# A decode attention block on one core: the exps' own semaphore, the first exps placed behind the second pair's evictions, and TensorE's loop placed at a slot of a fetch block

## The chip, the cores and the metric

The kernel runs on one core of one Trainium2 chip. The metric is the device time of one execution in microseconds. The core has five engines that run their own instruction streams side by side and wait for one another through semaphores: TensorE (PE in the profile; PEld is its weight load), VectorE (DVE), ScalarE (ACT), GpSimd (POOL) and SyncE (SP, which here only issues transfers). 16 DMA engines move the data. Data lie in SBUF (128 partitions), matmul results in PSUM banks.

## The reference

One decode step: 8 sequences with one new token each, 32 heads with a cache of 4096 keys and values of 128 numbers, and a small MLP beside the attention. All inputs are bf16.

```
xn = layernorm(x)                                  # x: 8 x 1 x 640
q  = (xn @ wq) as 8 x 32 x 1 x 128
p  = softmax(q . k_cache * 128**-0.5)              # over 4096 keys, each head of each sequence
o  = p . v_cache, as 8 x 1 x 4096
h  = gelu(layernorm(xn) @ w1 + b1)
out = x + o @ wo + h @ w2 + b2
```

Nearly all of the work is reading the two caches: 8 x 32 x 4096 x 128 numbers of 2 bytes each, that is 268 MB of keys and as many of values.

## The kernel before

**Pairs.** The caches are worked through in 32 pairs, numbered `i` from 0 to 31. A pair is one sequence and 8 heads. Its keys are 8 MB and are spread over the 128 partitions: 16 partitions for each head, 256 keys of 128 numbers on each partition. Its values have the same layout. There are two key buffers (even and odd pairs) and one value buffer. Before the pairs stand the two layernorms, the query projection and the MLP, whose weights and results use parts of the same buffers.

**What one pair does.** The scores of the first 176 keys of a partition are made on VectorE in three chunks (`dve_chunk`): multiply by the query, add the two halves, reduce. The scores of the last 80 are made on TensorE in ten groups of 8: `pe_T` transposes 8 blocks of keys into PSUM, `act_T` evicts the group to SBUF on ScalarE (tile KT_sb), `pe_QK` multiplies it by the queries (tile S_ps), and `dve_sel` picks each partition's own head from the result. `dve_max` finds the maximum and writes the bias NB. Then `act_exp` computes 8 exps on ScalarE (one for each head, tile P_sb, with their sums), `pe_RS` adds the sums over partitions, and `pe_PV` is the value product: 256 matmuls, each with its own weight load, summed in PV_ps. `act_O` copies the result out and `o_norm` divides on GpSimd. At the end `fin_wo` multiplies by the output weights in four parts, the first two of them ahead of the last value product.

**Order.** Every step is put on a time line by hand: `at(position, function, pair)`, 100 positions to a pair, and the calls are sorted by position. Within one engine the order of positions is the order of instructions. For pair i (o = 100 i) the transposes, evictions and score products stand at o to o + 42, the exps at o + 90, and the row sums and the value product at o + 148 and o + 150, that is behind the score products of pair i + 1. On TensorE one turn thus holds, in this order, the score products of pair i + 1 and then the value product of pair i.

**Transfers.** All cache loads are issued from SP's queue, in the order keys i + 1, values i, keys i + 2, values i + 1. `load_k(i)` waits until pair i - 2 is done with its buffer (transposes and VectorE's chunks). `load_v(i)` waits for the value product of pair i - 1 (`tk[("pv", i - 1)]`), as there is one value buffer. SP waits in order, so a load that waits holds back those behind it. The values of the last pair come in four parts.

**Semaphores.** Each engine has one counting semaphore (`act_s` for ScalarE), raised by the instructions that others wait for. A wait is left out where the waiting engine has already waited for a later count of the same semaphore (class `_Eng`). TensorE has a second semaphore for the row sums and the value products (`pe2`).

**Loops.** VectorE and ScalarE have pairs 2 to 31 as a loop of 15 turns (`_replay_loop`). TensorE has a loop of 32 turns over pairs (`_replay_pe`): from turn to turn the instructions must be the same and the waited counts must grow by one step. A turn has a first half (query matmul, transposes and score products of the next pair; in the last turn, under `If_eq`, two parts of the output product instead) and a second half (row sums, value product). To keep the counts of `act_s` regular from the first turn on, the kernel before has two copies that no one reads: `act_exp(-1)` writes oU_sb, and `act_qbc(32)` writes qbc_sb.

**The first pairs.** Pair 0's score products stand ahead of TensorE's loop; the loop's first turn holds pair 1's score products and pair 0's value product. On ScalarE the exps of pair 0 stood at position 90, ahead of pair 1's evictions at 100 to 142.

Of the kernel before, what the change touches and what calls it, by code (L numbers as in the profile page):

```python
# [11 lines left out]
ACT = mybir.ActivationFunctionType  # L12
# [92 lines left out]
def _emit(e, call, wait=None, turn=None):  # L105
    name, a, k, inc = call
    a = [x.at(x.i if turn is None else turn) if isinstance(x, _Slot) else x for x in a]
    if name == "wait_ge":
        e.wait_ge(a[0], a[1] if wait is None else wait, **k)
        return  # L110
    inst = getattr(e, name)(*a, **k)  # L111
    if inc is not None:
        inst.then_inc(*inc)


def _replay(e, calls):
    for call in calls:
        _emit(e, call)
# [10 lines left out]
def _steps(turns):  # L129

    body = turns[0]
    assert len({len(t) for t in turns}) == 1, [len(t) for t in turns]
    grow = []
    for j, (name, args, kw, inc) in enumerate(body):
        step = 0
        for r in range(1, len(turns)):
            name_r, args_r, kw_r, inc_r = turns[r][j]
            assert name_r == name and inc_r == inc and sorted(kw_r) == sorted(kw), (j, name, name_r)
            if name == "wait_ge":
                assert args_r[0] is args[0]  # L140
                if r == 1:
                    step = args_r[1] - args[1]
                assert args_r[1] == args[1] + r * step and args[1] > 0 and step >= 0, (j, args, args_r)
            else:
                assert [_same(x) for x in args_r] == [_same(x) for x in args], (j, name)
                assert [_same(kw_r[x]) for x in sorted(kw)] == [_same(kw[x]) for x in sorted(kw)], (j, name)
        grow.append(step)
    return grow
# [14 lines left out]
def _replay_pe(e, calls, head, mid, end, late):  # L163

    n = len(head)
    first = [calls[a:b] for a, b in zip(head, mid)]
    second = [calls[a:b] for a, b in zip(mid, head[1:] + [end])]
    g1, g2 = _steps(first[:-1]), _steps([[c for c in t if not _late(c, late)] for t in second])
    _replay(e, calls[:head[0]])
    with e.bass.Fori(1, n + 1, engines=OrderedEngineSet([e.engine])) as r:  # L170
        reg = e.to_reg(r)
        with e.If_lt(reg, n):
            for call, step in zip(first[0], g1):
                _emit(e, call, call[1][1] + (r - 1) * step if step else None, r)
        with e.If_eq(reg, n):
            _replay(e, first[-1])
        g = iter(g2)
        for call in second[0]:
            if _late(call, late):
                e.wait_ge(call[1][0], (r >> (n.bit_length() - 1)) * 16 + 1)  # L180
            else:
                step = next(g)
                _emit(e, call, call[1][1] + (r - 1) * step if step else None)
    assert n & (n - 1) == 0
    _replay(e, calls[end:])


def _late(call, late):
    return call[0] == "wait_ge" and any(call[1][0] is x for x in late)


def bass_parallel_sum__gqa_block_cached__mixer_channel_mlp__decode_kernel(
# [17 lines left out]
    HS = 8  # L210
# [3 lines left out]
    NQ = NHQ * B  # L214
# [14 lines left out]
    def jp_of(i):  # L229
        return 80  # L230
# [16 lines left out]
    with ExitStack() as es:  # L247
# [3 lines left out]
        sem = lambda name: es.enter_context(nc.semaphore(name))  # L251
# [38 lines left out]
        qbc_sb = sb("qbc_sb", [P, 2, DH], BF)  # L290
        oT_sb = sb("oT_sb", [P, H, B], BF)
        oU_sb = sb("oU_sb", [P, 2, HS], F32)
        ident_bf = sb("ident_bf", [P, P], BF)
        mask_sb = sb("mask_sb", [P, HS], F32)
        off_sb = sb("off_sb", [P, HS], F32)
# [25 lines left out]
        assert H * B + (FB + 1) * B <= 384  # L321

        pe, dve, act, sp, pool = (_Eng(sem(f"{n}_s")) for n in ("pe", "dve", "act", "sp", "pool"))
        pe2 = _Eng(sem("pe2_s"))
        ld_s = [_Dma(sem(f"ld_s{s}")) for s in range(3)]
        ld_x, ld_b1, ld_b2, ld_wq, ld_w1, ld_w2a, ld_w2b, st_o = (
            _Dma(sem(n)) for n in ("ld_x", "ld_b1", "ld_b2", "ld_wq", "ld_w1", "ld_w2a", "ld_w2b", "st_o"))
# [3 lines left out]
        tk = {}  # L331
        prog = []

        def at(pos, fn, *a):
            prog.append((pos, len(prog), fn, a))
# [161 lines left out]

        def act_qbc(i):
            act.wait(tk.get(("ym", i - 2)))
            if i == NQ:  # L500
                act.sig(act.activation(qbc_sb[:, i % 2, 0:HS], off_sb[:, :], ACT.Copy))
                return
            QBB.use(act)
            tk[("qb", i)] = QBB.used(act, act.sig(act.activation(
                qbc_sb[:, i % 2, :], QB_ps[:, 0:DH], ACT.Copy)))
# [83 lines left out]

        def act_exp(i):  # L590
            s = i % 2
            if i < 0:
                act.wait(tk["mask"])
                act.sig(act.activation(oU_sb[:, s, :], off_sb[:, :], ACT.Copy))
                return
            act.wait(tk[("nb", i)], tk.get(("pv", i - 1)))
            for h in range(HS):
                last = act.activation(P_sb[:, h, :], Sd_sb[:, s, :], ACT.Exp, bias=NB_sb[:, s, h:h + 1],
                                      scale=SCALE, accum_out=rs_sb[:, h:h + 1])
            tk[("exp", i)] = act.sig(last)  # L600

        def pe_RS(i):
            pe.wait(tk[("exp", i)])
# [24 lines left out]

        def act_O(i):
            if i < 0:  # L630
                tk[("oU", i)] = PVB.used(act, act.sig(act.activation(oU_sb[:, i % 2, :], off_sb[:, :], ACT.Copy)))
                return
            PVB.use(act)
            tk[("oU", i)] = PVB.used(act, act.sig(act.activation(oU_sb[:, i % 2, :], PV_ps[:, 0:HS], ACT.Copy)))
# [42 lines left out]
        Q = 100.0  # L677
# [22 lines left out]
        for i in range(NQ):  # L700
            o = i * Q
            last = i == NQ - 1
            if i:
                at(o - 51, load_k, i)
            at(o + 50, load_v, i)
            at(o - 52, qrep, i)
            at(o - 2, k_ready, i)
            at(o - 11, pe_qbc, i)
            at(o - 10.5, act_qbc, i)
            nt = jp_of(i) // TPB  # L710
            w = 42.0 / nt
            for t in range(nt):
                at(o + w * t, pe_T, i, t)
                at(o + w * (t + 0.4), act_T, i, t)
                at(o + w * (t + 1.5), pe_QK, i, t)
            at(o + 2, dve_chunk, i, 0)
            at(o + 26, dve_chunk, i, 1)
            at(o + 52, dve_sel, i, 0)
            at(o + 55, dve_sel, i, 1)
            at(o + 58, dve_chunk, i, 2)  # L720
            at(o + 84, dve_max, i)
            at(o + 90, act_exp, i)
            at(o + Q + 48, pe_RS, i)
            at(o + Q + 57, dve_rinv, i)
            at(o + Q + 50, pe_PV, i)
            if not last:
                at(o + Q + 71, act_O, i)
            at(o + Q + 75, o_norm, i)
        at(-10, act_exp, -1)
        at(NQ * Q - 10.5, act_qbc, NQ)  # L730
        at(57, dve_rinv, -1)
        at(71, act_O, -1)
        at(75, o_norm, -1)
        o = NQ * Q
# [32 lines left out]
        @block.tensor  # L767
        def _(e):
            _replay_pe(e, pe.calls, head, mid, end[0], [d.sem for d in ld_vl])
# [40 lines left out]
```

## Time and profile before

| what | value |
|---|---|
| timed runs, us | 1292.55, 1292.06, 1290.01 (median 1292.06) |
| the profiled execution, us | 1290.35, with a span of 1288.5 |
| granted TensorE clock, mean | 0.576 |
| busy, share of the span | PE 52%, DVE 85%, ACT 37%, POOL 6% |
| DMA | 551.99 MB, mean 428 GB/s |
| chain that ended last | DMA 78%, PE 18%, ACT 1%, DVE 1% |

The span runs from the first instruction to the last; the execution's time has a little more around it. The chain is followed back from the last instruction, at each step to what released it. "issue" is time in which an engine waited for nothing that the profile shows. Value loads take 75% of the chain and value products 17%. An engine may be idle or busy without any effect on the time where it isn't on that chain, and a chain may run through work that another wait would replace at once.

Instruction fetches of TensorE show as a queue of their own (q8) in the table of DMA queues. All engines' program lines carry the number of the one line that replays the recorded calls, so groups are told apart by the tile that they write.

### The profile page before, as it was taken

Reading aid. Unit: us, or ns where it says so; the run is one execution under the profiler, and the core shown is the slowest. Engines: PE = TensorE matmul, PEld = TensorE weight load, DVE = VectorE, ACT = ScalarE, POOL = GpSimd, SP = SyncE. Lnnn points to the kernel's source line nnn. Section 1 sums busy time; section 2 is a strip of 40 time slices with the busy share of each in tenths; the row PEclk is TensorE's granted clock in tenths of the full one; section 3 lists DMA queues with packets and bytes.
Section 4 is the critical chain, followed back from the end, with each engine's and each line's share of the span. In section 5 each row is a group of like instructions: output and inputs, shape, how many; then the busy total and the mean of one; then the engine's idle time right before and its main releaser. Section 6 shows DMA issues by size and latency. Waiting matters only on the chain.

```text
span 1288.5 us, 34287 instructions
## 1 busy us (share of the span) xinstructions
PE 672.9 (52%) x13904; PEld 573.5 (45%) x13904; DVE 1089.4 (85%) x663; ACT 475.4 (37%) x906; POOL 77.4 (6%) x107
## 2 busy tenths in 40 slices
PE   4346544664544664544664644664644654544654
PEld 4235443553443553433553533553534543534544
DVE  1899888988888988888988888988888988888983
ACT  1344423344423344423344423344423344423341
POOL 0000000000000000000000000000000000000000
PEclk9955555666656666555565555556555665556565
DMA  9998999999999999999999999999999999999998
GB/s 398 443 425 373 446 433 423 442 437 423 431 448 423 427 452 423 423 454 425 423 454 425 423 450 429 423 442 437 423 434 444 425 429 446 427 425 450 427 402 347
DMA packets 14547, 551.99 MB, mean 428 GB/s; under 512 B 1276, under 2 KB 5445, under 8 KB 5574
## 3 DMA queue, kind: packets, MB, share of 16 engines
q1 hardware_dynamic: 14464, 551.79, 99.4%
q8 instruction: 9, 0.15, 0.0%
q10 hardware_dynamic: 70, 0.03, 0.0%
q14 instruction: 4, 0.03, 0.0%
HBM read 551.80 MB, written 0.01 MB: 428 GB/s over the span
## 4 chain that ended last, share of the span: by engine, by line
DMA 78%; PE 18%; ACT 1%; DVE 1%; issue 1%; SPq 0%; POOL 0%; ACTq 0%; DVEq 0%
DMA S_sb<-in_A_v_cache_dram 75%; PE PV_ps L111 17%; DMA S_sb<-in_A_k_cache_dram 3%; PE TR_ps L111 1%; ACT KT_sb L111 1%; DVE S_sb L111 0%; DVE Sd_sb L111 0%; PE S_ps L111 0%; ACT P_sb L111 0%; SPq L111 0%; PE ACC_ps L111 0%; PE CH_ps L111 0%; DVE S_ps L111 0%; DVE mx_sb L111 0%; PE QB_ps L111 0%
## 5 line engine op out<-in xcount | busy, mean ns | idle before, releaser
L111 PE MATMUL TR_ps<-ident_bf,S_sb 128*128 128x128 bf16 (+1 forms) x2570 | 339.9, 276 | 381.9 <-POOL kr_sb L111 367.4
L111 DVE TENSOR_TENSOR S_sb<-S_sb,qbc_sb 128x7552 bf16<-128x7552 bf16 (+1 forms) x96 | 388.8, 4050 | 143.7 <-DMA S_sb<-in_A_k_cache_dram 143.5
L111 PEld LDWEIGHTS TR_ps<-ident_bf,S_sb 128*128 (+2 forms) x2570 | 244.0, 103 | 439.4 <-issue 364.6
L111 DVE TENSOR_REDUCE Sd_sb<-S_sb 128x59 f32<-128x3776 bf16 (+1 forms) x96 | 390.2, 4065 | 3.3
L111 ACT ACTIVATE KT_sb<-TR_ps 128x1024 bf16<-128x1024 bf16 x320 | 326.9, 1023 | 124.1 <-PE TR_ps L111 112.6
L111 PE MATMUL PV_ps<-P_sb,S_sb 128*128 128x8 bf16 x8192 | 225.5, 175 | 157.8 <-DMA S_sb<-in_A_v_cache_dram 149.1
L111 PEld LDWEIGHTS PV_ps<-P_sb,S_sb 128*128 128x128 bf16 x8192 | 222.3, 103 | 161.0 <-DMA S_sb<-in_A_v_cache_dram 152.2
L111 ACT ACTIVATE P_sb<-Sd_sb,NB_sb 128x256 bf16<-128x256 f32 x256 | 126.2, 494 | 224.6 <-DVE NB_sb L111 224.6
L111 DVE TENSOR_TENSOR S_sb<-S_sb 128x3776 bf16<-128x3776 bf16 (+1 forms) x96 | 202.9, 2114 | 3.3
L111 ACT ACTIVATE oU_sb<-PV_ps 128x8 f32<-128x8 f32 x31 | 5.5, 177 | 403.8 <-PE PV_ps L111 403.8
L111 PE MATMUL S_ps<-qrep_sb,KT_sb 128*128 128x8 bf16 x2560 | 122.0, 177 | 41.8 <-ACT KT_sb L111 38.3
L111 PEld LDWEIGHTS S_ps<-qrep_sb,KT_sb 128*128 128x128 bf16 x2560 | 91.5, 102 | 73.3 <-ACT KT_sb L111 40.0
L111 POOL TENSOR_TENSOR oT_sb<-oU_sb,ri_sb 128x8 bf16<-128x8 f32 x31 | 60.5, 1953 | 397.8 <-ACT oU_sb L111 381.2
L111 ACT ACTIVATION_READ_ACCUMULATOR P_sb<-Sd_sb,NB_sb 128x1 f32 x256 | 47.7, 186 | 0.0
L111 POOL COPY qrep_sb<-qT_sb 128x128 bf16<-128x128 bf16 x32 | 12.8, 399 | 461.1 <-PE S_ps L111 441.4
L111 DVE TENSOR_REDUCE Sd_sb<-S_ps 128x40 f32<-128x320 f32 x64 | 31.5, 492 | 2.2
L111 DVE TENSOR_TENSOR S_ps<-S_ps,mask_sb 128x320 f32<-128x320 f32 x64 | 31.4, 490 | 1.7 <-PE S_ps L111 1.7
L111 POOL MEMSET kr_sb<- 128x1 f32 x32 | 3.1, 98 | 323.2 <-DMA S_sb<-in_A_k_cache_dram 323.2
L111 PE MATMUL CH_ps<-rs_sb,ones_f 128*128 128x8 f32 x64 | 16.0, 323 | 11.0 <-ACT P_sb L111 7.1
L111 PEld LDWEIGHTS CH_ps<-rs_sb,ones_f 128*128 128x128 f32 x64 | 13.2, 257 | 14.0 <-issue 14.0
L111 PE MATMUL CH_ps<-S_sb 128*128 128x8 bf16 (+1 forms) x244 | 12.0, 181 | 5.4 <-DMA S_sb<-in_A_wq_dram 4.7
L111 ACT ACTIVATE qbc_sb<-QB_ps 128x128 bf16<-128x128 f32 x32 | 8.9, 277 | 16.1 <-PE QB_ps L111 16.1
(46 smaller groups left out, 104.6 us busy)
## 6 DMA issues: line engine op xcount, KB each, us to landing
S_sb<-in_A_wq_dram SPq DMA_DIRECT2D x1, 5120.0 KB, 15.6
S_sb<-in_A_k_cache_dram SPq DMA_DIRECT2D x1, 4448.0 KB, 43.1
S_sb<-in_A_k_cache_dram SPq DMA_DIRECT2D x1, 3744.0 KB, 33.1
S_sb<-in_A_v_cache_dram SPq DMA_DIRECT2D x1, 3072.0 KB, 12.8
S_sb<-in_A_wo_dram SPq DMA_DIRECT2D x1, 2560.0 KB, 32.5
S_sb<-in_A_v_cache_dram SPq DMA_DIRECT2D x1, 2560.0 KB, 18.5
S_sb<-in_B_w_dram SPq DMA_DIRECT2D x1, 2160.0 KB, 20.2
S_sb<-in_B_w_dram SPq DMA_DIRECT2D x1, 2080.0 KB, 25.2
```

Source lines behind the costliest of these rows:

```text
L111: inst = getattr(e, name)(*a, **k)
```

## The change

The loop of TensorE gets a fixed place: its first instruction is put at slot 100 of a block of 256 instructions. The exps signal on a semaphore of their own, `act2_s`, through a second recorder `act2`; they are still recorded in ScalarE's stream, in the same order as its other calls. The exps of pair 0 move from position 90 to position 145, that is behind the evictions of pair 1; those of the other pairs stay at o + 90. The two copies that no one reads go, and the wait for the mask that the first of them held moves to `act_O(-1)`.

```diff
-    with e.bass.Fori(1, n + 1, engines=OrderedEngineSet([e.engine])) as r:
+    with e.bass.Fori(1, n + 1, engines=OrderedEngineSet([e.engine]), head_slot={e.engine: 100}) as r:
...
-        pe2 = _Eng(sem("pe2_s"))
+        pe2, act2 = _Eng(sem("pe2_s")), _Eng(sem("act2_s"))
...
         def act_qbc(i):
             act.wait(tk.get(("ym", i - 2)))
-            if i == NQ:
-                act.sig(act.activation(qbc_sb[:, i % 2, 0:HS], off_sb[:, :], ACT.Copy))
-                return
             QBB.use(act)
...
         def act_exp(i):
             s = i % 2
-            if i < 0:
-                act.wait(tk["mask"])
-                act.sig(act.activation(oU_sb[:, s, :], off_sb[:, :], ACT.Copy))
-                return
             act.wait(tk[("nb", i)], tk.get(("pv", i - 1)))
             for h in range(HS):
                 last = act.activation(P_sb[:, h, :], Sd_sb[:, s, :], ACT.Exp, bias=NB_sb[:, s, h:h + 1],
                                       scale=SCALE, accum_out=rs_sb[:, h:h + 1])
-            tk[("exp", i)] = act.sig(last)
+            tk[("exp", i)] = act2.sig(last)
...
         def act_O(i):
             if i < 0:
+                act.wait(tk["mask"])
                 tk[("oU", i)] = PVB.used(act, act.sig(act.activation(oU_sb[:, i % 2, :], off_sb[:, :], ACT.Copy)))
                 return
...
-            at(o + 90, act_exp, i)
+            at(o + 90 if i else o + Q + 45, act_exp, i)
...
-        at(-10, act_exp, -1)
-        at(NQ * Q - 10.5, act_qbc, NQ)
```

## The prediction

> **What bounds the kernel now.** I read the page's slices and queues first, then the chain of waits, the timelines of the queues, and a table of short windows.
>
> ```profile
> DMA  9998999999999999999999999999999999999998
> q1 hardware_dynamic: 14464, 551.79, 99.4%
> q8 instruction: 9, 0.15, 0.0%
> ```
>
> ```profile
> 105.94 21.78 DMA S_sb<-in_A_v_cache_dram
> 127.72 0.05 issue
> 127.77 7.04 PE PV_ps L111 x256
> 134.82 31.63 DMA S_sb<-in_A_v_cache_dram
> 166.45 0.05 issue
> 166.50 7.04 PE PV_ps L111 x256
> ```
>
> The transfers bound it: 551.79 MB keep the DMA engines busy 99.4% of the span. The second fence is the chain (start, length): value load, value product, next value load. A steady pair takes 38.70 us (134.82 to 173.55 and on), half of it, 19.35 us, for each 8 MB load. The chain seems to say that TensorE's 7.04 us matter. They don't: a value load issued onto a dry queue at 105.94 landed 21.78 us later, one issued at 134.82 needed 31.63 us, since a key load stood ahead of it. So each steady value load is issued 31.63 - 21.78 = 9.85 us before it is needed. Nothing TensorE, ScalarE or VectorE gains in a steady pair counts; only a dry queue does. There is one, at the fourth slice:
>
> ```profile
> 72.47 4.04 ACT P_sb L111 x16
> 76.52 0.92 ACT KT_sb L111
> ...
> 89.17 0.34 issue
> 89.52 0.59 PE CH_ps L111 x2
> 90.11 0.75 PE PV_ps L111 x28
> 90.86 4.63 issue
> 95.49 3.57 PE PV_ps L111 x128
> 99.06 4.01 issue
> 103.07 2.85 PE PV_ps L111 x100
> ```
>
> ```profile
> 100.00:102.00 2.00, 0.00 (x0) 0.50 1.11 467
> 102.00:104.00 2.00, 0.93 (x34) 0.50 0.15 66
> 104.00:106.00 2.00, 1.91 (x72) 0.50 0.03 8
> 106.00:108.00 2.00, 1.53 (x10) 0.50 1.55 524
> ```
>
> The first is the chain again: the first value product is broken twice by "issue", time in which TensorE waited for no semaphore: 4.63 us after 28 matmuls, 4.01 us after 128 more. 128 matmuls with their weight loads are 256 instructions, and the instruction queue q8 moved 0.15 MB in 9 packets, 16 KB each, 64 bytes for each of 256: TensorE ran out of code at two block boundaries. In the second fence (window, length, PE busy, granted clock, share of packets begun, GB/s) few packets begin between 102 and 106: key load 2 (issued at 70.88) is done, and value load 1 is issued only at 105.94, after the broken product.
>
> **Size of the hole.** Value load 1 landed at 127.72. The last part of key load 2 landed at 105.02 (landing events). Without a hole value load 1 ends 105.02 + 19.35 = 124.37: 3.35 us to be had on the engine that is last; the first engines were done at 103.09 and lost up to 4.76. Taking the busy time of packets in half-microsecond steps from 102 to 108, 3.4 of 16 engines' us are missing. From 21.78, the load must be issued by 124.37 - 21.78 = 102.59 to close the hole.
>
> **The change, part by part.**
>
> *The first exps behind the second pair's evictions.* Today ScalarE starts exp 0 at 72.47 (when VectorE has NB) and the 10 evictions of pair 1 wait behind it until 76.42, though their keys are there at 66.33 and TensorE has two transposed groups ready. Moved, pair 1's transposes, evictions and score products run at once. A steady pair needs 13.95 us from the keys' signal to the last score product (POOL's signal 147.13, its next copy 161.08). So the last score product ends at 66.33 + 13.95 = 80.3 instead of 89.17, and the last eviction at about 79.9. Behind it stand the eight exps, 4.04 us, and perhaps the exps' table load, 1.28 us (today at 60.43, in idle time): done at 83.9 to 85.2. I take 85.2. Who waits for them: the row sums and the product on TensorE, and VectorE's exp waits two pairs on, which come after 106. Value load 0, issued at 32.00, lands 53.6 us later, at 85.6. So data allow the product at about 85.8, 4.3 us earlier than today's 90.11.
>
> *TensorE's code.* Fetches of the instruction queue begin at 86.0, 93.0, 100.5 and 104.2; each takes 1.0 to 1.1 us. The first block boundary inside the product was free 95.49 - 89.2 = 6.3 us after the block before was entered, the second 103.07 - 95.49 = 7.6 us; so one block is fetched ahead, on entering a block, and takes a mean of 6.94 us while loads fill the engines. A block of product runs 3.57 us. Counting the records of one turn, there are 673 instructions from the loop's head to the product's first, with 242 skipped ones (output weights), and 515 from there to the loop's end. Head at slot 100: 100 + 673 = 773 = 3 x 256 + 5, so the product does begin a block, to within my count; today, 57 instructions ahead of a boundary, the head is at about slot 38. But 513 instructions of product begun at slot 0 to 5 don't end in two blocks: the last few stand in a third. The block before the product is entered by pair 1's last score product, about 12 instructions before the first half ends, at 80.0. Then: first product block 80.0 + 6.94 = 86.9 (after exps and data, so it decides), second 93.9, third 100.8, end 100.9. Bounds by 6.3 and 7.6: 98.9 and 102.8; where the third isn't needed, 93.9 + 3.6 = 97.5. I take 100.9, as the count puts instructions in the third block. That is ahead of 102.59 by 1.7 us: the hole closes, with 0.2 us left at the far bound. The placement itself gains nothing then: with the boundaries where they are today, the chain would be two fetches and 100 matmuls, 80.4 + 2 x 6.94 + 2.85 = 97.1.
>
> The Trainium skill, "Runtime: NRT & Kernel Launch", section "Instruction fetch mechanics", says that code is fetched ahead in 16 KiB blocks and that crossing a block is mostly hidden. Here the blocks agree, and 4.63 and 4.01 us of stall say that it isn't hidden under full loads. By that rule the product would run from 85.8 to 92.9, and the hole would close all the same.
>
> *A semaphore of their own.* The same instructions signal. Waits that one count covered may now need one more wait on VectorE and TensorE in each pair. The nearest rows, TensorE's wait and register steps, are about 0.1 us each; twice per pair that is 0.2 us, or nothing. VectorE waits 5.97 us for keys at 147.19, TensorE has 9.85 us: hidden; without that cover 31 x 0.2 = 6 us. I take 0.
>
> *Removed copies* on ScalarE: one beside the evictions of pair 0, 0.20 us at 58.84, one at 1258.04, 0.21 us, with exps only at 1265.84: 0.
>
> *Entering the loop* by a branch: 0 to 0.3 us at 59.3, while TensorE waits for keys until 66.33: 0.
>
> *What is late next.* Key load 3 needs VectorE's products of pair 1 (105.04), which don't move: issued at 105.1 behind value load 1, which runs until 124.4. Pair 2's exps wait for VectorE until 106.7 as today; its last score product ends at 123.1, the product starts at 123.8, and its values land at 124.4. The saving passes on, by 0.6 us; lost cover there would first be taken from the 9.85.
>
> **Sum.** Gain 3.35 (2.8 at an issue of 103.1, 4.1 if fast engines set the end) against the profiled run's 1290.35 (span 1288.5): 1287.0. The three timed runs have a median of 1292.06, 1.71 above the profiled one. The mean of all four is 1291.24, and my forecast is 1291.24 - 3.35 = 1287.9. What this kernel's measurement can tell from no change is 0.2%, 2.6 us, so the gain is just over it.
>
> **Rivals.**
>
> *The chain of fetches is too slow.* Three fetches at 8 us, or an entry 2 us later, put the issue at 104: the gain falls to 3.35 - 1.4 = 1.9, 1289.3, no change. For it: three steps in a row with only 1.7 us to spare. Against it: both measured fetches are under 7.6.
>
> *A fourth fetch stands in the chain*, because the branch over the skipped code leads to a block that isn't the next one: 80.0 + 4 x 7.6 = 110.4. It costs from an issue of 105.94 on: 110.4 - 105.94 = 4.5 us, 1295.7, slower. Against it: my count has branch and product in neighbouring blocks.
>
> *The loop no longer stays in the instruction store.* The body is 1188 instructions: from slot 38 it ends in a fifth block, from slot 100 in a sixth. If fetches come in every turn, three boundaries at (4.63 + 4.01) / 2 = 4.32 are 13.0 us; it decides from 9.85 on, so 3.1 us in each of 31 turns, 97 us, 1388. For it: one block more. Against it: no packet of q8 between 105 and 1285, so five blocks and the one fetched ahead are held. The skill's same section speaks of two lines of 16 KiB, which would refetch in every turn already now; the trace contradicts that, and its other figure for TensorE, 128 KiB, would hold eight.
>
> *The reordering does nothing*, as value load 0 (85.6) holds the product anyway: even then the product starts 4.3 us earlier, and the hole closes with an end at 101.6.
>
> **Chances.** Hole closed 0.66 (1287.9; with scatter of the runs 1285.2 to 1290.2; in about one in eight of these cases under 2.6 us); chain too slow 0.20 (1289 to 1291.5, mostly no change); fourth fetch 0.08 (to 1296); refetching loop 0.06. The fourth rival goes with the first case. So faster 0.61, same 0.26, slower 0.13. The range 1285.2 to 1291.8 holds the first two, about 0.8.
>
> **What would show it.** In the changed profile: evictions of pair 1 from about 67.7, exps at 80 to 85, last score product at 80.3; value load 1 issued between 97 and 103; no window with few packets at 102 to 106; key load 2 and value load 1 landing 19.4 us apart; later pairs still 38.70 us. Wrong if value load 1 is issued after 103, if q8 shows packets in steady turns, or if pairs change their length.

## The result, and the profile after

The changed kernel takes 1288.09 us (median of 15 runs, 1287.50 to 1288.48), the kernel before, run beside it, 1292.06 us (15 runs, 1289.76 to 1292.89). The ratio is 0.9974, with a 95% interval from 0.9966 to 0.9982: 0.26% faster. The profiled execution went from 1290.35 to 1288.09 us, its span from 1288.5 to 1286.2.

The runs of the kernel before stand in two groups, 1289.8 to 1290.5 (7 runs) and 1292.1 to 1292.9 (8 runs). Their mean is 1291.36, that of the changed kernel 1288.03: 3.3 us less. The profile of before is of the lower group, so the two profiles show only 2.26 us of it.

From the page of the changed kernel, the DMA slices and the queues:

```profile
DMA  9999999999999999999999999999999999999998
q1 hardware_dynamic: 14464, 551.79, 99.6%
q8 instruction: 9, 0.15, 0.0%
```

The fourth slice no longer falls under 9. The chain of waits in the same stretch as shown of before (start, length, what):

```profile
86.68 1.75 issue
88.43 0.60 PE CH_ps L111 x2
89.03 3.31 PE PV_ps L111 x124
92.33 3.60 issue
95.93 3.56 PE PV_ps L111 x128
99.49 3.73 issue
103.23 0.27 PE PV_ps L111 x4
103.49 0.02 issue
103.51 21.77 DMA S_sb<-in_A_v_cache_dram
...
132.36 32.86 DMA S_sb<-in_A_v_cache_dram
```

The first value product now meets three stalls for code: ahead of the row sums, after 124 matmuls, and ahead of the last 4. Value load 1 is issued at 103.51 instead of 105.94. The last line is new: value load 2 took 32.86 us, where the steady loads of before took 31.58 to 31.73, and one (load 12) 32.04. The windows that were nearly empty before (window, length, PE busy, granted clock, share of packets begun, GB/s):

```profile
102.00:104.00 2.00, 0.25 (x4) 0.50 0.38 164
104.00:106.00 2.00, 0.62 (x4) 0.50 1.57 524
```

ScalarE, timeline: the last eviction of pair 1, then the table load, then the first exp.

```profile
79.61 1.02 ACT L111 ACTIVATE KT_sb<-TR_ps 128x1024 bf16<-128x1024 bf16 x1 [0.21 <-PE TR_ps L111]
80.65 1.28 ACT L111 ACT_TABLE_LOAD   x1
81.94 0.51 ACT L111 ACTIVATE P_sb<-Sd_sb,NB_sb 128x256 bf16<-128x256 f32 x1
```

### The profile page after: what moved, and what is told of

Its sections match the earlier page's. It is cut to its first block, busy times and chain, and to the rows that moved or that the text cites. A ratio compares the mean times of both kernels' runs of the same rounds, so it can differ in the third digit from the quotient of the medians.

```text
span 1286.2 us, 34348 instructions
## 1 busy us (share of the span) xinstructions
PE 671.8 (52%) x13904; PEld 571.3 (44%) x13904; DVE 1089.4 (85%) x663; ACT 475.3 (37%) x904; POOL 84.2 (7%) x107
## 3 DMA queue, kind: packets, MB, share of 16 engines
q1 hardware_dynamic: 14464, 551.79, 99.6%
## 4 chain that ended last, share of the span: by engine, by line
DMA 78%; PE 17%; DVE 2%; issue 1%; ACT 1%; SPq 0%; POOL 0%; ACTq 0%; DVEq 0%
DMA S_sb<-in_A_v_cache_dram 75%; PE PV_ps L111 17%; DMA S_sb<-in_A_k_cache_dram 3%; DVE S_sb L111 1%; DVE Sd_sb L111 1%; ACT KT_sb L111 1%; SPq L111 0%; PE TR_ps L111 0%; PE ACC_ps L111 0%; PE S_ps L111 0%; PE CH_ps L111 0%; DVE S_ps L111 0%; DVE mx_sb L111 0%; PE QB_ps L111 0%; ACT out_sb L111 0%
## 5 line engine op out<-in xcount | busy, mean ns | idle before, releaser
L111 POOL TENSOR_TENSOR oT_sb<-oU_sb,ri_sb 128x8 bf16<-128x8 f32 x31 | 64.5, 2080 | 397.5 <-DVE S_sb L111 327.4
L111 POOL COPY qrep_sb<-qT_sb 128x128 bf16<-128x128 bf16 x32 | 15.6, 487 | 453.7 <-PE S_ps L111 434.0
```

## The experiments

The theory behind them: the time goes with the hole in the transfers after the first value product; the reordering closes it; the fixed place of the loop only sets how many code blocks that product has to wait for. The rivals give the gain to the place, or to the semaphore.

**The change without the fixed place** (e1):

```diff
-    with e.bass.Fori(1, n + 1, engines=OrderedEngineSet([e.engine]), head_slot={e.engine: 100}) as r:
+    with e.bass.Fori(1, n + 1, engines=OrderedEngineSet([e.engine])) as r:
```

> The changed kernel without the loop's fixed place: exps of pair 0 behind pair 1's evictions, own semaphore. Theory (the gain is the closed DMA hole, the reordering closes it, the place only sets how many code blocks the first product waits for): product starts at 86.7 when the exps are done, waits for two blocks (81.1 + 7.6 = 88.7 and 96.2) and ends with 100 matmuls at 99.1; value load 1 issued at 99.1, ahead of 102.6, so value load 1 lands at 124.5 instead of 125.28: 0.7 us below the changed kernel, 1287.4. Rival (the place makes the gain): 1290 to 1292, value load 1 issued after 105.

Measured: 1286.02 us (5 runs, 1285.87 to 1286.31), ratio to the kernel before 0.9955 (0.9941 to 0.9968): below the changed kernel by 2.07 us, more than the 0.7 expected. Its chain of waits:

```profile
85.59 0.24 issue
85.83 0.56 PE CH_ps L111 x2
86.39 0.75 PE PV_ps L111 x28
87.14 1.22 issue
88.35 3.56 PE PV_ps L111 x127
91.91 3.75 issue
95.66 2.86 PE PV_ps L111 x101
98.52 0.02 issue
98.53 25.73 DMA S_sb<-in_A_v_cache_dram
...
131.34 31.62 DMA S_sb<-in_A_v_cache_dram
```

Two boundaries fall into the product, after 28 and 155 matmuls, as in the kernel before. The load is issued at 98.53 and takes 25.73 us: it stands behind key load 2, so the queue never ran dry. The reordering closes the hole, and the place takes something back.

**The fixed place alone**, the kernel before with `head_slot={e.engine: 100}` (e2):

> The kernel before with its loop's head at slot 100 and nothing else. Theory: three blocks wait behind pair 1's last score product at 89.2, so 96.8, 104.3, 111.8; value load 1 issued at 112.0 instead of 105.94, and the hole grows by 6.1 us: 1296 against 1290.35 of the profiled run. Rival (the place makes the gain): 1288. Second rival (the first product is hidden, the hole has another cause): 1290 to 1292.

Measured: 1291.91 us (11 runs, 1291.45 to 1292.52), ratio 1.0002 (0.9993 to 1.0011). The place gains nothing; the expected 1296 was wrong as well. The kernel before has two groups of times, this one has a single one, and even its fastest run is longer than the lower group. The chain:

```profile
94.80 0.61 issue
95.41 0.60 PE CH_ps L111 x2
96.01 3.33 PE PV_ps L111 x125
99.34 4.02 issue
103.36 3.58 PE PV_ps L111 x128
106.94 0.15 issue
107.09 0.27 PE PV_ps L111 x3
107.36 0.02 issue
107.37 21.79 DMA S_sb<-in_A_v_cache_dram
```

The third block cost 0.15 us, not the 3.9 us I had put in. Its packet began at 104.86, 1.5 us after the block before it was entered, when key load 2 was still moving on one of the 16 engines only. The fetch that would have widened the hole is quick as soon as the hole is there. So value load 1 came 1.4 us later than in the profile of before, not 6.1.

**The head 12 slots earlier** (e3), `head_slot={e.engine: 88}` in the changed kernel:

> The changed kernel with the head 12 slots earlier, so that the first product ends inside its second block and needs no third one. Theory: blocks at 88.5 and 96.0, end at 96.0 + 3.6 = 99.6, value load 1 issued at 99.6, hole closed: 0.7 us below the changed kernel, 1287.4. Rival (the third block isn't what keeps 0.9 us of the hole open): 1288.1 as the changed kernel.

Measured: 1286.11 us (5 runs, 1286.00 to 1286.41). The end of the product in the chain:

```profile
87.98 3.56 PE PV_ps L111 x127
91.54 4.30 issue
95.84 3.53 PE PV_ps L111 x126
99.37 0.02 issue
99.38 25.15 DMA S_sb<-in_A_v_cache_dram
```

The issue time came as expected (99.38 for 99.6), and the time fell by 2.0 us, not by 0.7: the third block costs more than the rest of the hole. All 32 turns now keep to five blocks, as without the fixed place.

**The semaphore alone** (e4): no fixed place, and

```diff
-            at(o + 90 if i else o + Q + 45, act_exp, i)
+            at(o + 90, act_exp, i)
```

> The changed kernel with the exps of pair 0 back at their old position and no fixed place: what is left is the exps' own semaphore and the two removed copies. Theory: as the kernel before, value load 1 issued at about 106, 1290 to 1292.5. Rival (the semaphore makes the gain, as waits on the common count were late): 1288.

Measured: 1290.23 us (11 runs, 1289.44 to 1292.63, in two groups like the kernel before), ratio 0.9994 (0.9985 to 1.0003); value load 1 issued at 105.81. Neither the semaphore nor the two removed copies move the time.

**The head 7 slots earlier** (e5), `head_slot={e.engine: 93}`, which takes the two losses of slot 100 apart:

> The changed kernel with the head 7 slots earlier: the first product's last matmul is the last instruction of its second block, and only the loop's closing branch stands in a third. Value load 1 is then issued at 99.5 and the hole is closed as at slot 88 (1286.11), but every turn still enters the third block. Theory (slot 100 loses 2.0 us to slot 88 in two parts, 0.8 by the hole and 1.2 by the ninth code packet, which is fetched in the second turn under full load and makes one DMA engine late for good): 1287.3, a code packet at about 135, and the last landing of value load 2 about 39.9 us behind that of value load 1 instead of 38.7. Rival (the hole alone is what slot 100 loses): 1286.1.

Measured: 1287.31 us (7 runs, 1287.14 to 1287.56). The size is the theory's, the place isn't: nothing happens in the second turn. Chain of waits around the ninth packet of code, which begins at 329.4:

```profile
286.24 31.64 DMA S_sb<-in_A_v_cache_dram
...
324.95 33.00 DMA S_sb<-in_A_v_cache_dram
...
365.03 31.64 DMA S_sb<-in_A_v_cache_dram
```

One value load, the one issued and not yet landed at 329.4, takes 33.00 instead of 31.64 us, and the loss stays to the end. Each load lands in 16 parts. Up to value load 6 they land within 1.72 us; of value load 7 fifteen parts land within 1.70 us and the last one 1.38 us after them, and so it stays with every load that follows.

**The kernel before, three more runs** (e6, no edit), for its two groups of times:

> The kernel before once more, for a profile of its other time: its runs stand in two groups, 1289.8 to 1290.7 and 1291.1 to 1293.4, while the changed kernel's stand within 1.0 us. Theory (a code fetch in the first product waits for one more 64 KB packet of its DMA engine, 2.4 us): in the longer group a stall of 6 to 7 us instead of 4.0 or 4.6, and value load 1 issued at about 108. Rival (the longer group comes from the run's later part): value load 1 issued at 105.9 in both, the difference later. A run of the shorter group shows the stalls of the profile before again.

> As for the first of these three: the kernel before, in the longer group a longer stall and value load 1 at about 108, or (rival) the same stalls and a difference later.

> As for the first of these three: the kernel before, in the longer group a longer stall and value load 1 at about 108, or (rival) the same stalls and a difference later.

Measured: 1293.03, 1290.51 and 1292.26 us, so two of the upper group and one of the lower. The second issued value load 1 at 106.06, with the stalls of the profile before; the others at 108.48 and 108.36. The chain of the first:

```profile
89.53 1.87 issue
91.40 0.59 PE CH_ps L111 x2
91.99 0.75 PE PV_ps L111 x28
92.74 5.02 issue
97.76 3.56 PE PV_ps L111 x128
101.32 4.29 issue
105.61 2.85 PE PV_ps L111 x100
108.46 0.02 issue
108.48 21.82 DMA S_sb<-in_A_v_cache_dram
```

The 2.4 us are there, but not in one stall of 6 to 7 us: 1.5 us come ahead of the row sums (1.87 for 0.34), 0.7 in the two stalls within the product, and 0.4 is a later last score product. The packet for the row sums' block began at 88.46 (88.50 in the third run), against 86.01 and 86.07 in the lower group. That is 2.4 us, and the median duration of a 64 KB packet is 2.42 us, which fits a wait for one more packet on that DMA engine. The wait itself isn't in the records, so that much is argued.

**Both on one chip** (e7 the changed kernel, e8 without the fixed place):

> The changed kernel once more, on one chip with the kernel without the fixed place. Theory: 1288.1, of which 0.7 us is the rest of the hole (value loads 0 and 1 land 39.4 us apart) and 1.2 us the ninth code packet (one pair of later value loads lands 39.9 us apart, all others 38.70). Rival (the 2 us between the two came from different chips): the two medians agree within 0.5 us.

> The changed kernel without the loop's fixed place once more, on one chip with the changed kernel. Theory: 1286.0, every two value loads in a row land 38.70 us apart, and no code packet comes between 101 us and the end. Rival: within 0.5 us of the changed kernel.

Measured: 1287.93 us (11 runs, 1287.45 to 1288.44) and 1286.14 us (5 runs, 1286.02 to 1286.29): 1.8 us apart, ranges that don't touch. The ninth code packet of e7 came at 175.2. Loads 0 and 1 of e8 landed 39.04 us apart where 38.70 was expected; there was still no hole, as value load 1 landed 19.35 us after key load 2 (124.73 after 105.38), which is what a load takes in a steady pair, but key load 2 itself ended 0.46 us later than in e1.

The distances between the last landings of successive value loads, from the landing events, put all profiles on one scale; a loss that stays shows as one distance over 38.70 us.

```
kernel               loads 0 to 1   largest later distance (load)   time, us
before                  42.08          39.14 (12)                    1290.35
before, upper (e6 a)    44.78          39.09 (12)                    1293.03
before, lower (e6 b)    42.21          39.08 (12)                    1290.51
before, upper (e6 c)    44.37          38.80 (12)                    1292.26
place alone (e2)        43.47          39.98 (2)                     1292.52
semaphore alone (e4)    42.09          39.11 (3)                     1290.22
changed                 39.40          39.93 (2)                     1288.09
changed (e7)            39.11          40.07 (3)                     1287.93
slot 93 (e5)            38.71          40.08 (7)                     1287.31
slot 88 (e3)            38.70          none over 38.78               1286.06
no fixed place (e1)     38.70          none over 38.78               1285.87
no fixed place (e8)     39.04          none over 38.78               1286.29
```

The times are those of the profiled executions. Against e1, the changed kernel's surplus is 0.70 + 1.23 = 1.93 us, its time 2.2 us more; slot 93's is 1.38, its time 1.4 us more. A later distance of 39.9 or more stands in the kernels whose loop enters a sixth block, and in no other, and it is the value load issued and not yet landed when the ninth code packet comes (136.7, 140.7, 175.2 and 329.4 in the four profiles; 1281 or later in all others). Each of the four packets begins 4.9 to 5.0 us after the closing branch of a turn of the loop (131.8, 135.7, 170.2 and 324.4 in the records of TensorE's branches).

## Why the prediction was right, and where it wasn't

**What bounds the kernel** held in every run: the hole and one late packet moved the time, steady pairs stayed at 38.70 us in all kernels, and single distances that were longer for another reason were so by 0.44 us at most.

**The reordering** was right in mechanism and size. The last score product ended at 81.1 (80.3 said), the exps at 86.0 (85.2, with the table load that did move behind the evictions), and later pairs took no harm: but for the one late load they stayed at 38.70 us, with VectorE's busy time at 1089.4 us as before (GpSimd's rose from 77.4 to 84.2 us, without effect on the time). Without the place, and with its semaphore, it closes the hole (e1, e8).

**The chain of code fetches** was right in form, block by block, and 2.6 us too short: 103.51 for 100.9. The second half's first block was entered at about 80.7 (80.0 said), and the three blocks were usable 7.7, 7.5 and 7.3 us after the one before was entered, where the mean of two stalls gave 6.94; the last four matmuls add 0.27. So the issue came 0.9 us after 102.59, beyond even my far bound of 102.8, and 0.70 us of the hole was left. That the third block decides was seen; the margin was not as wide as put. So of the signs that were named, those for the hole failed. Value load 1 was issued after 103, which was put down as a sign of being wrong; few packets begin from 102 to 104 (a share of 0.38, where a full window has about 1); and value load 1 landed 20.06 us after key load 2 (105.22 to 125.28), not 19.4. The hole of 3.4 us shrank to 0.7 and did not close. A slip of naming besides: the exps that wait until 106.7 are pair 1's, not pair 2's.

**"The placement itself gains nothing"** was the step that fell short: it costs. I counted the three blocks for the first product and let the loop's sixth block pass as a matter of fitting. It fits, as q8 shows one packet from the second turn on. But, by the count of packets, the block that follows it is then fetched once while loads fill the engines, and a packet of q8 in a later turn was the other sign of being wrong. In the kernel before, the last packet of the first turn begins at 104.2, inside the hole, where it costs nothing, and the ninth comes at 1285. Here one engine is late for good: of value load 1 all 16 parts land within 0.58 us, of value load 2 fifteen within 0.54 us and the last one 1.22 us after them. The load lands 1.23 us late. Both parts of the place's cost together are the 1.8 to 2.1 us between e7 and e8, and between the first changed run and e1. The 97.1 us that I gave for boundaries where they were before turned out as 98.53.

**The sum.** The gain was put at 3.35 us against a mean of the known times. It came out at 3.3 us against the mean of 15 runs, but of other terms. Closing the hole is worth 4.2 us against the lower group of before (1290.2 to e1's 1286.0), near my bound of 4.1: by the landings 42.08 - 38.70 = 3.38 in the hole itself and 0.65 in three small later distances (loads 12, 23 and 30; in e1 none of them is over 38.75). Why these are longer in the kernel before was not tested. Against the upper group it is worth some 2.4 us more, which I took for scatter of the runs; over both groups that adds 1.2. From these 5.4 go 0.70 for the hole left and 1.23 for the late packet, 3.5 in all, for 3.3 measured. So a cost left out and a second group not recognised came near to cancelling each other: that 1287.9 came within 0.2 us of the result is luck in part.

**The rivals.** The chain that is too slow came true in part, by 0.9 us. A fourth fetch didn't come into the product. The loop was held, six blocks of it: the rival of refetching in every turn is out. That the semaphore counts is out by e4.

**What stays open.** In which turn the ninth packet comes: it follows the closing branch by about the 5 us by which other fetches follow the entry of a block, but in the second, third or seventh turn, in profiles whose code and early times are nearly the same. And why the fetch of the row sums' block is 2.4 us later in two of the four profiles of the kernel before (and, by the times, in about half of its runs), while kernels with the reordering keep within 1.0 us. In those the product waits for the exps at that time, which would hide it, but no run was made for it, and the place alone (e2), without the reordering, keeps within 1.1 us too.

## What to carry to other kernels

Where transfers bound a kernel, look for the place where the queue runs dry, work out by when the next load must be issued, and move only what stands ahead of that issue; here eight exps put behind ten evictions were worth 4 us against the lower group of before, and nothing else gained. A loop's place in its code blocks mattered here in its first turn, when code arrived while data loads filled the engines, and an extra block touched by the loop's end cost 1.2 to 1.4 us by its late packet alone. The version without the fixed place, at 1286.0 to 1286.1 us, is faster than both kernels, by 1.8 to 2.1 us than the changed one.

## What the runs showed of the hardware that wasn't expected

A code block of 16 KB was usable some 6.3 to 8.0 us after its predecessor was entered while loads filled the engines (7.3 to 7.7 in the changed kernel), and about 3.7 us after it where they stood dry (e2, 103.36 to 107.09, of which 3.58 us were matmuls anyway). In the changed kernel the packets for the second and third block of the product began 5.0 and 4.7 us after the block before was entered (93.45 and 100.67), in the dry case 1.5 us after. The transfer itself took 1.0 to 1.1 us in all three, and 1.3 to 1.5 us more passed until the block was used. So what full engines add lies ahead of the packet's start.

The Trainium skill, "Runtime: NRT & Kernel Launch", section "Instruction fetch mechanics", calls the crossing of a block mostly hidden. It isn't in a first pass under full load: 2.9 to 5.1 us of stall at each boundary in these profiles that no other wait covers, and none in later turns.

A single 16 KB packet of code made one of the 16 engines late by more than its own 1.0 to 1.1 us: the value load issued at that time landed 1.2 to 1.4 us later, and every load after it too, since the product starts only behind the last of a load's 16 parts (125.28 and 125.33 in the changed kernel).
